# The first batch's attention written out in one fixed order (Nyström attention and a gated MLP on one core)

## The chip, the cores and the metric

The kernel runs on one core of one Trainium2 chip. The metric is the device time of one execution in microseconds; less is better. Three runs of the kernel before gave 793.19, 793.43 and 793.94 us, a median of 793.43 us. In this document PE is the matrix engine (TensorE), PEld its weight loads, DVE is VectorE, ACT is ScalarE, POOL is GpSimd, and SP issues the DMAs.

## The reference

Eight batches of Nyström attention (8 heads, 576 tokens, head size 64, 32 landmarks) feed a gated MLP over all 4608 tokens.

```python
q_lm = q.reshape(B, H, m, S // m, D).mean(axis=3)      # m = 32 landmarks; k_lm likewise
A = sm(q, k_lm); Bm = sm(q_lm, k_lm); C = sm(q_lm, k)  # sm: softmax over the last axis
Z = Bm.T / (norm1(Bm) * norminf(Bm) + 1e-6)
for _ in range(6):
    Z = 2 * Z - Z @ Bm @ Z                             # Newton steps to a pseudo-inverse
x = (A @ Z @ C @ v)                                    # (B*S) x (H*D) = 4608 x 512
xn = x / sqrt(mean(x * x) + 1e-6) * rms_g              # one factor for each token row
out = (silu(xn @ w_gate) * (xn @ w_val)) @ w_out       # 512 -> 1536 -> 512
```

## The kernel before

**Stages.** Each batch's attention is handled in two groups g of four heads. The names to follow are these. `sums` adds up the landmarks (tile lmT, L574). `front` multiplies the scores (sC, sA), takes their maxima (L612 to L615), the exponentials on ACT (E, L618; eb, L622) and, in its inner `tail`, the sums' reciprocals and the transposed scores tA (L634). `soften` subtracts the row maxima of tA (L650 on DVE, L651 on POOL) and takes the exponential (L652). `weigh` normalises tA and transposes it to AT (L658 to L665). `turn` and `values` multiply by v (pCV, PV, L710). `newton_start` prepares the inverse (with a copy that spreads four sums over 128 columns, L849), `newton_first` and `newton_step` are the starting value and the six Newton steps (PV, L868 and L884; the last writes VF, L882). `newton_weights` makes W and the weights' factor WT. `second` multiplies out the attention (pO), squares it (sq, L953), finds each token's RMS factor with a bit trick and polynomial (L969 to L981), scales AT with it (L987, L989), and splits the result into a high and a low part, an (L991 on ACT, L992 on DVE). an is what the MLP multiplies.

**The MLP.** `mix_weights` folds WT into a pair of weight slices (pM, Mhi, Mlo); `mlp` multiplies them with an (psg, psv, 12 products for each of the two token halves), takes SiLU on ACT (L505), multiplies on DVE (L506) and splits the result h (L510, L511); `outs` multiplies h by w_out (pso). The MLP of the first half of the hidden units runs batch by batch, and the attention of the next two batches is laid between its products.

**The weights.** They come as pieces of 0.5 MB (tiles wraw), are decoded by two ACT passes (L185, L186) and finished by one DVE pass (L190) in `load_next`, one after another. A piece of gate or value weights is a quarter of a pair (tile wgv).

**What sets the order.** PE's order is fixed as written (`keep_in_program_order`). On the other engines a scheduler orders the instructions by data and priority, unless one is told to come after another (`issue_after`). A planner, the Mixer, deals out generators (`opening`, `first_inverse`, `first_second`, `decode`, later `steady`) by a running clock of costs; `until(chunk, n)` places a part of the second batch's attention behind the n-th product of the MLP. For the first batch the two urgent generators run at high priority, and `decode` (L1100) sends weight pieces and the second batch's first sums between them. `steady` places `sums(1, 1)`, that is the landmark sums of the second batch's second group, behind product 37 and behind the last weight piece finished until then (`early.last`, L796), and `front(1, 1)` behind product 46.

## Time and profile before

| | us |
|---|---|
| median of three runs | 793.43 |
| the profiled execution, whole | 792.78 |
| its span, first to last instruction | 791.0 |
| PE busy in the span | 767.7 (97%) |
| DVE, ACT, POOL busy | 567.5, 418.6, 182.1 |

The page of the profile gives the chain that ended last as 87% PE, with 4% DVE, 4% ACT and 2% DMA. All timeline times below are microseconds from the start of the span. "Idle before" in square brackets is the time in which the engine stood still before a row's instruction, with what ended it. Instructions in a row overlap a little: the distance from one start to the next is what a queue pays for one.

### The profile page before, as it was taken

The page shows a single profiled execution, that of the slowest core. Times are in us where ns is not written, and L with a number is a line of the kernel's source. Part 1 is how long each engine was busy: PE and PEld are TensorE (multiplying, and loading weights), DVE is VectorE, ACT ScalarE, POOL GpSimd, SP SyncE. Part 2 cuts the span into 40 slices and gives each one's busy share as a digit, 9 for nine tenths or more (in the row PEclk, how much of TensorE's full clock was granted, in tenths as well). Part 3 has the DMA queues.
Part 4 walks back from the last instruction along what each step waited for, and adds up shares of the span by engine and source line. Part 5 has one row for each costly group of instructions (what it writes and reads, how often), then busy time and mean ns, then how long its engine had stood idle before and what let it go on. Part 6 is the DMA issues. An engine that isn't in the chain of part 4 may idle for free.

```text
span 791.0 us, 17865 instructions
## 1 busy us (share of the span) xinstructions
PE 767.7 (97%) x7012; PEld 618.7 (78%) x7012; DVE 567.5 (72%) x1329; ACT 418.6 (53%) x923; POOL 182.1 (23%) x189
## 2 busy tenths in 40 slices
PE   7787999999999999999999999999999999999998
PEld 5465668778778778677778879797979797979796
DVE  7899787947969758688577574767576757766672
ACT  4578465535545455454474785555355444535450
POOL 1005220110210200200200004353334424433430
PEclk9999999999999999999999999999999999999999
DMA  9877461541652532621556541323332424151412
GB/s 320 310 241 221 142 220 61 189 133 33 198 180 93 183 130 70 191 80 53 167 168 211 168 137 41 132 94 145 94 145 68 158 80 159 54 184 56 171 41 80
DMA packets 55204, 110.83 MB, mean 140 GB/s; under 512 B 5456, under 2 KB 29008, under 8 KB 55120
## 3 DMA queue, kind: packets, MB, share of 16 engines
q1 hardware_dynamic: 55120, 109.69, 41.5%
q8 instruction: 55, 0.90, 0.5%
q14 instruction: 29, 0.24, 0.1%
HBM read 73.69 MB, written 35.98 MB: 139 GB/s over the span
## 4 chain that ended last, share of the span: by engine, by line
PE 87%; DVE 4%; ACT 4%; DMA 2%; issue 2%; SPq 0%; ACTq 0%; DVEq 0%
PE pso L115 38%; PE p L115 17%; PE psg L115 8%; PE psv L115 8%; PE pM L115 5%; PE pn L115 2%; PE pCV L115 2%; PE sC L115 2%; PE pO L115 1%; PE pss L115 1%; DMA qk<-in_k_dram 1%; PE sE L121 1%; DMA wrawo<-in_moe_w_out_dram 1%; PE pW L115 1%; DVE lmT L574 1%
## 5 line engine op out<-in xcount | busy, mean ns | idle before, releaser
L115 PE MATMUL pso<-wo,h 128*128 128x512 f32 x648 | 158.4, 396 | 0.0
L115 PEld LDWEIGHTS pso<-wo,h 128*128 128x128 f32 x648 | 118.6, 188 | 31.4 <-ACT E L618 4.2
L115 PE MATMUL pso<-lhio,h 128*128 128x512 f32 x432 | 139.2, 392 | 0.0
L115 PEld LDWEIGHTS pso<-lhio,h 128*128 128x128 f32 x432 | 81.1, 188 | 23.0 <-issue 5.9
L115 PE MATMUL p<-xb,Bwgv 128*128 128x288 f32 x560 | 90.8, 296 | 0.0
L115 PE MATMUL psg<-an,Mhi 128*128 128x288 f32 x384 | 85.3, 306 | 4.6 <-ACT s L505 2.5
L115 PE MATMUL pso<-lloo,h 128*128 128x512 f32 x216 | 84.4, 391 | 0.0
L115 PE MATMUL psv<-an,Mhi 128*128 128x288 f32 x384 | 83.9, 302 | 0.0
L115 PEld LDWEIGHTS p<-xb,Bwgv 128*128 128x128 f32 x560 | 81.3, 188 | 1.2
L413 POOL TENSOR_TENSOR s<-s,vv 128x576 f32<-128x576 f32 x40 | 57.4, 1434 | 98.5 <-DVE vv L455 95.6
L115 PEld LDWEIGHTS psg<-an,Mhi 128*128 128x128 f32 x384 | 61.9, 189 | 16.5 <-DVE WT L898 4.2
L115 PE MATMUL p<-xb,Bwo 128*128 128x288 f32 x392 | 70.1, 295 | 0.0
L115 PEld LDWEIGHTS psv<-an,Mhi 128*128 128x128 f32 x384 | 62.7, 191 | 2.1
L1123 ACT COPY ob<-pso 128x512 f32<-128x512 f32 x36 | 21.0, 589 | 74.5 <-PE pso L115 53.1
L115 PEld LDWEIGHTS p<-xb,Bwo 128*128 128x128 f32 x392 | 58.9, 188 | 1.2
L115 PE MATMUL psv<-an,Mlo 128*128 128x288 f32 x192 | 59.0, 307 | 0.0
L505 ACT ACTIVATE s<-psg 128x288 f32<-128x288 f32 x96 | 39.4, 410 | 36.0 <-PE psg L115 35.8
L115 PE MATMUL psg<-an,Mlo 128*128 128x288 f32 x192 | 58.3, 304 | 0.0
L651 POOL TENSOR_TENSOR tA<-tA,mA 128x576 f32<-128x576 f32 x16 | 18.3, 1164 | 170.3 <-DVE mA L650 170.3
L1185 DVE TENSOR_TENSOR obl<-obl,pso 128x512 f32<-128x512 f32 x36 | 24.7, 686 | 43.3 <-PE pso L115 43.3
L506 DVE TENSOR_TENSOR s<-s,psv 128x288 f32<-128x288 f32 x96 | 42.4, 446 | 11.0 <-PE psv L115 7.5
L510 ACT CAST h<-s 128x576 fp32r<-128x576 f32 x48 | 32.2, 670 | 28.2 <-DVE s L506 28.2
(185 smaller groups left out, 1479.0 us busy)
## 6 DMA issues: line engine op xcount, KB each, us to landing
xb<-ad SPq DMA_DIRECT2D x16, 1008.0 KB, 5.3
qk<-in_q_dram SPq DMA_DIRECT2D x16, 576.0 KB, 4.8
qk<-in_k_dram SPq DMA_DIRECT2D x16, 576.0 KB, 6.0
pd<-ob SPq DMA_DIRECT2D x36, 256.0 KB, 3.6
ad<-t SPq DMA_DIRECT2D x64, 144.0 KB, 1.8
obl<-pd SPq DMA_DIRECT2D x36, 256.0 KB, 2.7
out_dram<-obl SPq DMA_DIRECT2D x36, 256.0 KB, 2.1
vt<-in_v_dram SPq DMA_DIRECT2D x16, 512.0 KB, 5.7
```

What stands on the lines that cost most here:

```text
L115: tc.keep_in_program_order(nc.tensor.matmul(*args, **kw))
L121: tc.keep_in_program_order(nc.tensor.transpose(*args))
L413: kept(eng.tensor_mul(ss[f][:, e], ss[f][:, e], vv[f][:, e]))
L505: silu["last"] = nc.scalar.activation(s[:, cols], banks[0], AF.Silu).ins
L506: nc.vector.tensor_mul(s[:, cols], s[:, cols], banks[1])
L510: nc.scalar.copy(h[:, 0, TAIL:], s)
L574: fixed["sums", b] = nc.vector.tensor_reduce(lmT[:, z], loaded[b, g][z].rearrange("p h (m c) -> p h m c", c=LM), axis=AX.X, op=ALU.add,)
L651: nc.gpsimd.tensor_sub(tA, tA, mA.unsqueeze(2).broadcast_to([P, NB, M]))
L1123: nc.scalar.copy(ob, ps)
L1185: kept(nc.vector.tensor_add(ob, ob, ps))
```

## The change

**An order by hand.** The generators of the first batch are gone. `opening` now writes the first batch's attention, the first half of the second batch's (`Front(1, 0)`) and the first weight pieces as one list, and every instruction made with `own=pin` keeps its place on its engine's queue. `front` is cut into a class with the parts tops (maxima), exps, totals and turned; `soften` into lower and expose; `weigh` into shares and back; `load_next` into `begin` (the two ACT passes) and the `finish` that it returns (the DVE pass).

**What moves between engines (first batch only).** The scalings of pCV into PV and the copy of W go from DVE to ACT. The normalisation of tA (two multiplications) goes from DVE to POOL. The spreading copy in `newton_start` becomes a reduction over an axis of one element, still on DVE. The four banks of the second token half's pO, pss, pms come from the other PSUM pool.

**What moves in time.** Both groups' maxima come before the sums' reciprocals. The second batch's first sums are cut in two: the q half stands between Newton steps 1 and 2, the k half behind WT. AT is scaled and split by token halves (`row`, `high`, `low`). Six weight pieces pass ACT in the opening, ahead of the first products, where before it was nine; DVE finishes four of them ahead of the second batch's maxima (`tops`) and two behind the split of an. Two more pieces can be fetched ahead (spots wo2 and wo1). The first batch's SiLUs are put behind the last high part of an.

```diff
+        def begin(self, own=free):
...
+            def finish():
+                with tc.issue_after(self.then) if self.then else nullcontext():
+                    last = own(
+                        nc.vector.scalar_tensor_tensor(
+                            w.bitcast(U32),
+                            raw[..., 0].bitcast(U32),
+                            5,
+                            w.bitcast(U32),
+                            op0=ALU.logical_shift_right,
+                            op1=ALU.bitwise_or,
+                        )
+                    )
+                self.last = last.ins
...
-                    silu["last"] = nc.scalar.activation(s[:, cols], banks[0], AF.Silu).ins
+                    with behind(fixed["hi", 0].ins if very else None):
+                        silu["last"] = nc.scalar.activation(s[:, cols], banks[0], AF.Silu).ins
...
+            def turned(self, after=None, es=range(2)):
+                b, g, nt = self.b, self.g, state[self.b]
+                if nt["tA"][g] is None:
+                    nt["tA"][g] = ap.tile([P, NB, M], F32, name="tA", tag="tA", bufs=TAB)
+                with tc.issue_after(after) if after else nullcontext():
+                    for e in es:
+                        fixed["tA", b, g] = self.own(
+                            nc.vector.transpose(
+                                nt["tA"][g][:, e * (NB // 2) : (e + 1) * (NB // 2), :].rearrange("p n m -> p (n m)"),
+                                self.sA[e],
+                            )
+                        )
...
+        def shares(b, g, own=free):
+            tA = state[b]["tA"][g]
+            sumA = sm.tile([P, NB], F32, name="sumA", tag="sumA")
+            own(nc.vector.tensor_reduce(sumA, tA, axis=AX.X, op=ALU.add))
+            own(nc.vector.tensor_scalar_add(sumA, sumA, 1e-9))
+            rA = sm.tile([P, NB], F32, name="rA", tag="rA")
+            own(nc.vector.reciprocal(rA, sumA))
+            own(nc.gpsimd.tensor_mul(tA, tA, rA.unsqueeze(2).broadcast_to([P, NB, M])))
+
+        def back(b, g, own=free):
+            nt = state[b]
+            nt["AT"][g] = AT = ap.tile([P, S], F32, name="AT", tag="AT", bufs=ATB)
+            own(nc.vector.transpose(AT, nt["tA"][g].rearrange("p n m -> p (n m)")))
...
-            nc.vector.tensor_scalar_mul(nt["PV"][:, g, M:], pCV, nt["rs"][g][:, 0:1])
+            to, by = nt["PV"][:, g, M:], nt["rs"][g][:, 0:1]
+            if b:
+                nc.vector.tensor_scalar_mul(to, pCV, by)
+            else:
+                pin(nc.scalar.mul(to, pCV, by))
...
+            b, own = 0, pin
             for g in range(2):
-                sums(0, g, None if g else made.ins)
+                sums(b, g, None if g else made.ins, own=own)
+            one, two = fronts = [Front(b, g, own) for g in range(2)]
+            for _ in range(4):
+                early.fetch()
             for g in range(2):
-                tails.append(front(0, g))
+                load_qk(1, g)
+            for _ in range(4, NF1 + RAWS):
+                early.fetch()
+            for part in fronts:
+                part.tops()
+            for part in fronts:
+                part.exps()
+            one.turned()
+            one.totals()
+            two.turned(es=(0,))
+            two.totals()
+            turn(b, 0, 3, own)
+            turn(b, 1, 0, own)
+            start = newton_start(b, own)
+            BT, den = next(start)
+            p0 = bmm(BT, BT, M, "p0")
             for g in range(2):
-                tails[g](fixed["mx", 0, 1].ins)
-            yield 2.6, 0.0
-            for g in range(2):
-                turn(0, g, 4 - 4 * g)
-                soften(0, g)
-                yield 0.65, 0.0
-            for g in range(2):
-                values(0, g, 1 - g)
-                yield 0.85, 0.0
-            stage["front"] = stage["first"] = 0
+                values(b, g, 1 - g)
+                load_v(1, g)
+            for _ in range(2):
+                early.fetch()
+            newton_first(b, p0, den, own)
+            two.turned(es=(1,))
+            lower(b, 0, own=own)
+            newton_step(b, 0, own)
+            spare(2)
+            lower(b, 1, own=own)
+            newton_step(b, 1, own)
+            spare(2)
+            ends = [early.begin(own) for _ in range(2)]
+            expose(b, 0, own)
+            expose(b, 1, own)
+            ends.extend(early.begin(own) for _ in range(2))
+            sums(1, 0, zs=(0,), own=own)
+            newton_step(b, 2, own)
+            spare(2)
+            next(start, None)
+            shares(b, 0, own)
+            newton_step(b, 3, own)
+            spare(2)
+            shares(b, 1, own)
+            newton_step(b, 4, own)
+            spare(2)
+            back(b, 0, own)
+            newton_step(b, 5, own)
+            spare(2)
+            back(b, 1, own)
+            newton_weights(b, own)
+            spare(1)
+            parts = second(b, own)
+            next(parts)
+            sums(1, 0, zs=(1,), own=own)
+            next(parts)
+            ends.extend(early.begin(own) for _ in range(2))
+            for _ in range(4):
+                ends.pop(0)()
+            nxt = Front(1, 0, own)
+            load_qk(2, 0)
+            nxt.tops()
+            nxt.exps()
+            next(parts)
+            nxt.turned(es=(0,))
+            next(parts)
+            low_parts = mix_weights(early, 0, 0, True, own)
+            low_parts()
+            for _ in parts:
+                pass
+            nxt.turned(es=(1,))
+            nxt.totals()
+            for end in ends:
+                end()
+            early.after = fixed["hi", 0].ins
+            for name in ("front", "first", "newton", "wt", "second"):
+                stage[name] = 0
...
+            spread = sums.unsqueeze(2).broadcast_to([P, 4, M])
+            if b:
+                nc.vector.tensor_copy(sb, spread)
+            else:
+                own(nc.vector.tensor_reduce(sb, spread.unsqueeze(3), axis=AX.X, op=ALU.max))
...
+            if b:
+                nc.vector.tensor_copy(W, straight)
+            else:
+                own(nc.scalar.copy(W, straight))
...
-                po = [pa.tile([P, HS], F32, name="pO", tag="pa") for n in range(4)]
+                pool, tag = other if e else (pa, "pa")
+                po = [pool.tile([P, 512], F32, name="pO", tag=tag)[:, :HS] for n in range(4)]
...
+            def row(e, n=1):
+                cols = slice(e * HS, (e + n) * HS)
+                at = slice(e * (NB // 2), (e + n) * (NB // 2))
+                own(nc.vector.transpose(rT[:, cols].rearrange("p (n m) -> p n m", m=M), rb[:, at]))
+                for g in range(2):
+                    own(nc.vector.tensor_mul(ATs[g][:, cols], ATs[g][:, cols], rT[:, cols]))
+
+            def high(g, cols=slice(0, S)):
+                fixed["hi", b] = own(nc.scalar.copy(an[:, 0, g, cols], ATs[g][:, cols]))
+
+            def low(g, cols=slice(0, S)):
+                fixed["an", b] = own(
+                    nc.vector.tensor_sub(an[:, 1, g, cols], ATs[g][:, cols], an[:, 0, g, cols].bitcast(F32))
+                )
+
+            if b:
+                row(0, 2)
+                for g in range(2):
+                    high(g)
+                    low(g)
+            else:
+                for e in range(2):
+                    row(e)
+                    for g in range(2):
+                        high(g, slice(e * HS, (e + 1) * HS))
+                    for g in range(2):
+                        low(g, slice(e * HS, (e + 1) * HS))
+                hold.enter_context(tc.issue_after(fixed["an", 0].ins))
...
-        spots = itertools.chain([(wp, f"h{f}", 1) for f in range(NF1)], ring)
+        spots = itertools.chain(
+            [(wp, f"h{f}", 1) for f in range(NF1)], [(wp, f"wo{n}", 1) for n in (2, 1)], ring
+        )
...
-        def decode():
-            while early.then is None:
-                yield -0.3
-            yield from early.stream(WAIT0, 2)
-            sums(1, 0, early.then)
-            yield -WAIT0
-            early.then = fixed["sums", 1].ins
-            yield from early.stream(WAIT0, 3)
-
-        early.ahead, early.after = 2, fixed["eb", 0, 1].ins
-        mix.add(first_second(), True)
-        mix.add(first_inverse(), True)
-        mix.add(decode())
-        mix.drain(lambda: stage["newton"] >= 0)
-        with tc.issue_after(fixed[0].ins):
-            mix.add(steady())
-            mix.drain(lambda: stage["second"] >= 0)
-            mix.part()
+        opening()
+        early.ahead = 2
+        mix.add(steady())
+        mix.part()
```

**On DVE, in the Newton steps of the first batch.** Before, from the last row ahead of the third Newton step (PV) on:

```order
L190 SCALAR_TENSOR_TENSOR wgv_436<-wrawg_352,wgv_436 128x4x128
L884 SCALAR_TENSOR_TENSOR PV<-PV,pn 128x192
L665 STREAM_TRANSPOSE AT<-tA 128x576
L190 SCALAR_TENSOR_TENSOR wgv_436<-wrawv_354,wgv_436 128x4x128
L884 SCALAR_TENSOR_TENSOR PV<-PV,pn 128x192
L574 TENSOR_REDUCE lmT<-qk_360 128x64
```

Now, from the first step on:

```order
L1031 SCALAR_TENSOR_TENSOR PV<-PV,pn 128x192
L708 TENSOR_REDUCE mA<-tA 128x18
L1031 SCALAR_TENSOR_TENSOR PV<-PV,pn 128x192
L599 TENSOR_REDUCE lmT<-qk_247 128x64
L1031 SCALAR_TENSOR_TENSOR PV<-PV,pn 128x192
L1008 TENSOR_TENSOR Bs<-Bm,nden 128x64
```

The sums lmT of the second batch (L574, now L599) stood behind the fourth step of PV; one of the two now stands ahead of the third.

**On ACT, from the split of an to the first h.** Before:

```order
L991 CAST an<-AT 128x576 x2
L505 ACT_TABLE_LOAD
L505 ACTIVATE s<-psg 128x288
L687 COPY ET<-sE 128x512
L688 COPY EL<-sF 64x128
L505 ACTIVATE s<-psg 128x288 x2
L510 CAST h_740<-s 128x576
L185 ACTIVATE wrawv_751<-wrawv_751 128x512
```

Now:

```order
L1132 CAST an<-AT 128x288 x4
L194 ACTIVATE wrawg_257<-wrawg_257 128x512
L756 COPY ET<-sE 128x512
L196 ACTIVATE wgv_575<-wrawg_257 128x4x128
L757 COPY EL<-sF 64x128
L528 ACT_TABLE_LOAD
L528 ACTIVATE s<-psg 128x288
L194 ACTIVATE wrawv_259<-wrawv_259 128x512
L528 ACTIVATE s<-psg 128x288
L196 ACTIVATE wgv_575<-wrawv_259 128x4x128
L194 ACTIVATE wrawg_261<-wrawg_261 128x512
L533 CAST h_748<-s 128x576
```

Five passes over weight pieces (L194, L196: pieces 257, 259 and 261) now stand among the first SiLUs (L528) and ahead of the first h (L533), where there was none.

**On DVE, from the second pair's last weight pieces to the scores of the second batch's second group.** qk_363 and qk_250 are that group's q and k; its scores are sC in the row `mx<-sC`. Before:

```order
L190 SCALAR_TENSOR_TENSOR wgv_781<-wrawg_374,wgv_781 128x4x128
L506 TENSOR_TENSOR s<-s,psv 128x288
L574 TENSOR_REDUCE lmT<-qk_363 128x64
L506 TENSOR_TENSOR s<-s,psv 128x288
L574 TENSOR_REDUCE lmT<-qk_363 128x64
L511 TENSOR_TENSOR h_740<-s,h_740 128x576
L506 TENSOR_TENSOR s<-s,psv 128x288
L190 SCALAR_TENSOR_TENSOR wgv_781<-wrawv_751,wgv_781 128x4x128
L283 TENSOR_TENSOR Mlo<-pM,Mhi 128x512 x2
L612 TENSOR_REDUCE mx<-sC 128x1
```

Now:

```order
L204 SCALAR_TENSOR_TENSOR wgv_575<-wrawg_257,wgv_575 128x4x128
L529 TENSOR_TENSOR s<-s,psv 128x288 x2
L204 SCALAR_TENSOR_TENSOR wgv_575<-wrawv_259,wgv_575 128x4x128
L534 TENSOR_TENSOR h_748<-s,h_748 128x576
L204 SCALAR_TENSOR_TENSOR wgv_756<-wrawg_261,wgv_756 128x4x128
L529 TENSOR_TENSOR s<-s,psv 128x288
L305 TENSOR_TENSOR Mlo<-pM,Mhi 128x512 x2
L204 SCALAR_TENSOR_TENSOR wgv_756<-wrawv_398,wgv_756 128x4x128
L599 TENSOR_REDUCE lmT<-qk_250 128x64 x2
L204 SCALAR_TENSOR_TENSOR wgv_756<-wrawg_400,wgv_756 128x4x128
```

The two sums lmT stood behind the first and the second product s; now they stand behind three products, three finished pieces and the low parts of the mixed weights, Mlo.

## Rows read from the trace of the kernel before

**Rows 1.** Windows table: us, busy us (x) by engine, granted clock, DMA share, GB/s

```profile
0.00:44.11 44.11, 31.41 (x465) 20.91 (x465) 34.47 (x96) 23.90 (x58) 4.75 (x14) 1.00 0.86 299
44.11:47.65 3.54, 3.35 (x13) 3.03 (x14) 3.54 (x6) 2.21 (x3) 0.00 (x0) 0.52 0.66 234
...
60.95:63.50 2.55, 0.09 (x1) 0.00 (x1) 2.55 (x9) 2.52 (x5) 0.35 (x2) 1.00 0.92 337
63.50:67.90 4.40, 4.40 (x68) 3.56 (x68) 4.38 (x15) 3.90 (x9) 1.55 (x3) 0.63 0.46 137
...
102.50:791.00 688.50, 683.87 (x5948) 558.60 (x5937) 482.43 (x1121) 354.10 (x783) 160.78 (x155) 1.00 0.37 124
```

**Rows 2.** Timeline, DVE: start us, us, engine, line, operation, shape, count [idle before]

```profile
17.82 1.12 DVE L849 COPY nsb<-nsum 128x128 f32<-128x128 f32 x1
...
20.39 0.23 DVE L868 TENSOR_TENSOR PV<-p,nden 128x64 f32<-128x64 f32 x1
...
25.50 0.35 DVE L884 SCALAR_TENSOR_TENSOR PV<-PV,pn 128x192 f32<-128x192 f32 x1
...
30.08 0.47 DVE L882 SCALAR_TENSOR_TENSOR VF<-PV,pn 128x128 f32<-128x128 f32 x2
...
35.84 0.46 DVE L612 TENSOR_REDUCE mx<-sC 128x1 f32<-128x288 f32 x1 [2.96 <-PE sA L115]
...
42.05 1.43 DVE L989 TENSOR_TENSOR AT<-AT,rT 128x576 f32<-128x576 f32 x2
...
64.47 0.87 DVE L857 TENSOR_TENSOR nden<-nnm 128x2 f32<-128x2 f32 x1
```

**Rows 3.** Timeline, DMA queue of SP

```profile
12.42 0.87 SPq L561 DMA_DIRECT2D qk<-in_q_dram  x1
```

**Rows 4.** DMA issues in 12.3 to 13.3 us: count, KB, us to landing

```profile
qk<-in_q_dram SPq DMA_DIRECT2D x1, 576.0 KB, 9.2
```

**Rows 5.** Timeline, ACT

```profile
32.78 1.32 ACT L953 ACTIVATE sq<-pO 128x288 f32<-128x288 f32 x4 [3.93 <-PE pO L115]
...
35.49 0.70 ACT L185 ACTIVATE wrawv<-wrawv 128x512 f32<-128x512 int8 x1
...
40.01 0.50 ACT L618 ACTIVATE E<-sC,mx 128x288 f32<-128x288 f32 x1
...
43.37 1.25 ACT L991 CAST an<-AT 128x576 fp32r<-128x576 f32 x2
...
57.28 1.28 ACT L618 ACT_TABLE_LOAD   x1 [1.42 <-DVE mx L615]
```

**Rows 6.** Timeline, PE

```profile
32.01 2.84 PE L115 MATMUL pO<-AT,W 32*64 32x288 f32 x32 [0.16 <-DVE W L897]
...
44.11 0.61 PE L115 MATMUL psg<-an,Mhi 128*128 128x288 f32 x1 [1.26 <-ACT an L991]
...
54.01 0.43 PE L115 MATMUL sC<-qk,lmT 64*32 64x288 f32 x1
...
63.50 0.53 PE L115 MATMUL psg<-an,Mhi 128*128 128x288 f32 x2 [2.46 <-ACT s L505]
...
68.40 1.09 PE L115 MATMUL pM<-wgv,WT 64*32 64x512 f32 x16
```

**Rows 7.** Groups by line, DVE, 21 to 60 us: xcount | busy us, mean ns

```profile
L574 DVE TENSOR_REDUCE lmT<-qk 128x64 f32<-128x1152 f32 x4 | 5.4, 1344 | 0.0
...
L190 DVE SCALAR_TENSOR_TENSOR wgv<-wrawg,wgv 128x512 uint32<-128x512 uint32 x6 | 4.1, 681 | 0.0
```

**Rows 8.** Groups by line, ACT, 35 to 60 us

```profile
L281 ACT CAST Mhi<-pM 128x512 fp32r<-128x512 f32 x4 | 2.1, 593 | 0.0
...
L505 ACT ACTIVATE s<-psg 128x288 f32<-128x288 f32 x4 | 1.7, 416 | 1.9 <-PE psg L115 1.9
```

**Rows 9.** Timeline, POOL

```profile
16.59 2.28 POOL L651 TENSOR_TENSOR tA<-tA,mA 128x576 f32<-128x576 f32 x2 [3.20 <-DVE mA L650]
...
64.16 1.16 POOL L663 TENSOR_TENSOR tA<-tA,rA 128x576 f32<-128x576 f32 x1 [2.10 <-ACT EL L688]
```

More of the change, by code (lines that the diff above doesn't have):

```diff
@@ L273, in mixed_banks, with mix_weights @@
         return ps
-    def mix_weights(wts, b, pair, late=False):
+    def mix_weights(wts, b, pair, late=False, own=free):
         ps = mixed_banks(wts, b, pair)
@@ L280, in mix_weights @@
         for g in range(G):
-            nc.scalar.copy(hi[:, g], ps[g])
+            own(nc.scalar.copy(hi[:, g], ps[g]))
             if not late:
@@ L288, in low_parts @@
                 mm(ps[g], minus, hi[:, g], start=False, stop=True, skip_group_check=True)
-                nc.scalar.copy(lo[:, g], ps[g])
+                own(nc.scalar.copy(lo[:, g], ps[g]))
         return low_parts
@@ L568, in load_v, with sums @@
             loaded[b, g, "v"] = (vt, vt2)
-        def sums(b, g, after=None):
-            lms[b, g] = lmT = sm.tile([P, 2, 2, M], F32, name="lmT", tag="lmT", bufs=2)
+        def sums(b, g, after=None, zs=range(2), own=free):
+            if (b, g) not in lms:
+                lms[b, g] = sm.tile([P, 2, 2, M], F32, name="lmT", tag="lmT", bufs=2)
             with tc.issue_after(after) if after else nullcontext():
-                for z in range(2):
-                    fixed["sums", b] = nc.vector.tensor_reduce(
-                        lmT[:, z],
-                        loaded[b, g][z].rearrange("p h (m c) -> p h m c", c=LM),
-                        axis=AX.X,
-                        op=ALU.add,
-                    )
@@ new lines, in sums, with __init__, tops @@
+                for z in zs:
+                    fixed["sums", b] = own(
+                        nc.vector.tensor_reduce(
+                            lms[b, g][:, z],
+                            loaded[b, g][z].rearrange("p h (m c) -> p h m c", c=LM),
+                            axis=AX.X,
+                            op=ALU.add,
+                        )
+                    )
+        class Front:
+            def __init__(self, b, g, own=free):
+                self.b, self.g, self.own = b, g, own
+                lmT, qk = lms.pop((b, g)), loaded.pop((b, g))
+                pool, tag = (pa, "pa") if b or not g else (pg, "pg")
+                sC = [pool.tile([P, 512], F32, name="sC", tag=tag) for e in range(2)]
+                sA = [pool.tile([P, 512], F32, name="sA", tag=tag) for e in range(2)]
+                for e in range(2):
+                    for h in range(4):
+                        for z, bank, at in ((1, sC[e], rho(g, h)), (0, sA[e], pos(g, h))):
+                            mm(
+                                bank[rows(at), :HS],
+                                lmT[half(h), 1 - z, h // 2, :],
+                                qk[z][half(h), h // 2, e * HS : (e + 1) * HS],
+                                start=True,
+                                stop=True,
+                            )
+                psB = sC[1][:, HS : HS + M]
+                for h in range(4):
+                    mm(
+                        psB[rows(rho(g, h)), :],
+                        lmT[half(h), 0, h // 2, :],
+                        lmT[half(h), 1, h // 2, :],
+                        start=True,
+                        stop=True,
+                    )
+                self.sC = [s[:, :HS] for s in sC]
+                self.sA = [s[:, :HS] for s in sA]
+                self.psB = psB
+                self.mx = sm.tile([P, 3], F32, name="mx", tag="mx")
+                self.ss = sm.tile([P, 3], F32, name="ss", tag="ss")
+                self.rs = sm.tile([P, 2], F32, name="rs", tag="rs")
+            def tops(self, after=None):
+                mx, own = self.mx, self.own
@@ L648, in soften, with front, lower @@
+        def front(b, g, after=None, late=None):
+            made = Front(b, g)
+            made.tops(after)
+            made.exps()
+            made.totals()
+            made.turned(late or after)
+        def lower(b, g, after=None, own=free):
+            tA = state[b]["tA"][g]
             mA = sm.tile([P, NB], F32, name="mA", tag="mA")
             with tc.issue_after(after) if after else nullcontext():
-                nc.vector.tensor_reduce(mA, tA, axis=AX.X, op=ALU.max)
-            nc.gpsimd.tensor_sub(tA, tA, mA.unsqueeze(2).broadcast_to([P, NB, M]))
@@ L652, in soften @@
[L652 to L666 removed]
+                own(nc.vector.tensor_reduce(mA, tA, axis=AX.X, op=ALU.max))
@@ L674, in spare, with turn @@
             idle(pg.tile([P, 512], F32, name="psw", tag="pg")[:, :P], n)
-        def turn(b, g, more=0):
+        def turn(b, g, more=0, own=free):
             E = state[b]["E"][g]
@@ L686, in turn @@
             EL = ap.tile([2 * M, P], F32, name="EL", tag="EL", bufs=2)
-            nc.scalar.copy(ET, sE)
-            last = nc.scalar.copy(EL, sF)
+            own(nc.scalar.copy(ET, sE))
+            last = own(nc.scalar.copy(EL, sF))
             if (b, g) == (1, 1):
@@ L938, in nystrom_moe_kernel, with second @@
         fixed = {}
-        def second(b):
+        def second(b, own=free):
             nt = state.pop(b)
             W, ATs = nt["W"], nt["AT"]
+            other = (pa, "pa") if b else (pg, "pg")
             sqs = []
```

328 lines of the change are left out of this document (130 added, 198 removed).

## The prediction

> **What bounds the kernel now.** I read the windows table first, since a share of 97% over the span says little about a change that is all in the first tenth of it. From 102.50 us to the end PE is busy 683.87 of 688.50 us at a granted clock of 1.00 [rows 1]. The order of PE's instructions behind that point is the same in both kernels, so what the change is worth is how much earlier or later PE gets there. Up to 44.11 us PE only serves the first batch's attention (31.41 us busy, most of it small products and fillers), and the first product of the MLP, psg, starts at 44.11 [rows 6]. From there PE is dense, with three blemishes that the reader finds in the same table: 44.11 to 47.65 at a clock of 0.52, a standstill of 2.46 us that ends at 63.50, and 63.50 to 67.90 at 0.63 [rows 1, 6]. Granted levels are 1.2 and 2.4 GHz; 0.52 is nearly all at the lower one. The standstill has its cause on ACT: the exponentials of the second batch's second group wait for its maxima, then load their table (1.28 us, from 57.28 on), and the SiLU that frees psg stands behind them [rows 5, 6].
>
> So I ask two questions: when does psg start now, and which wait between 44 and 68 us ends last then. I followed each engine's queue in the new order, with durations and pitches from the trace of before.
>
> **Part 1, up to the first psg.** Before, the six Newton updates pace this part: the start value PV at 20.39, the third update at 25.50, the sixth (VF) at 30.08, so 1.53 us each at the end [rows 2]. Three things ahead of the start value go: two scalings of pCV move to an idle ACT, the reductions of tA move behind it, and the copy nsb, 1.12 us for 128 columns, becomes a reduction that doesn't wait for POOL. The start comes 0 to 2.9 us earlier; from the rows around the copy I take 2.0 or more. Then the q half of the second batch's sums, now pinned ahead of the third update, decides: q is issued at 12.42 and takes 9.2 us to land [rows 3, 4], so 21.6, and the sum takes 1.34 [rows 7]. The third update starts at 22.95 in place of 25.50. If the start value doesn't come earlier, this gain is nil; if the transfer lands sooner, it is 2.9 at most. VF follows at 22.95 + 3 x 1.53 = 27.5 (before 30.08).
>
> From VF to the first square, sq, it was 2.70 us (30.08 to 32.78) [rows 2, 5], with the copy W on DVE; on an idle ACT it costs its own length only, and DVE has two finishes fewer in the way: 2.5, so 30.0. Eight squares take 2.7 (32.78 to 35.49), to 32.7. Before, eight decoding passes stood behind them on ACT, 35.49 to 40.01, so 0.565 a pass; four stand there now, to 35.0. From the first exponential E at 40.01 to the first high part of an at 43.37 it was 3.36 [rows 5]: ACT is ready at 38.3. DVE is the later one. The k half of the sums and four finishes of 0.68 [rows 7] lie ahead of the maxima mx, which start at 33.3 (before 35.84). From mx to an it was 43.37 - 35.84 = 7.53; half of the scaling (1.43 for two [rows 2]), half of the transposition rT, one transposition tA and the second batch's reciprocals now stand behind the first half of an, which I put at 1.8 together: 33.3 + 5.7 = 39.0, and the first psg at 39.5. **That is 4.6 us earlier than 44.11.** The normalisation on POOL has slack here: AT stands behind the fifth update now.
>
> About the POOL work the row shows this: the copy nsb ended at 18.94, when a subtraction pair on POOL (16.59 + 2.28) ended too, and nden, a product of two columns, took 0.87 us from 64.47 on and ended at 65.34, within 0.02 of a POOL multiplication [rows 2, 9]. The Trainium skill, "SBUF — State Buffer", section "Who interferes with whom", says that a DVE copy or scalar operation in a two-port mode, or one with two inputs in SBUF, and GpSimd exclude each other for a whole instruction, and that a tensor_reduce never contends on trn2; the trace agrees. By that rule the reduction nsb is free, but the normalisation of the first group on POOL may hold up the second group's small sumA operation. The sum would be up to 0.4 higher (most of one 1.16 us multiplication is covered by the sums ahead). I leave it out of the sum and keep 0 to 1.16 in the range.
>
> **Part 2, from psg to the scores of the second group.** Before, this stretch had 44.11 to 54.01 with no wait on PE. The scores sC and sA of the second batch's second group need two landmark sums, and these now stand on DVE behind finishes whose passes have yet to run on ACT. From the first 12 products (39.5 to 42.6, at half clock as before) and the turn of E, ET can be copied at 43.4. From there ACT's queue to the last pass that the sums wait for is: ET and EL 0.65, a table load 1.28, eight passes at 0.565, 4.52, three SiLUs with some 0.95 between starts in all (0.42 each alone), one h 0.57, two Mhi 1.06 (0.59 each alone) [rows 5, 8]. That is 9.0, so 52.5. One finish of 0.68 and two sums of 1.34 on DVE [rows 7] give 55.8, and the scores end at 56.9. Before they started at 54.01 and were done at 55.1. **So here 6.4 us go back: 1.8 later than before.** PE, whose order is fixed, stands still for some 3.4 us ahead of the first scores and 1.3 between those of the q half and the k half. Passes left out of the opening's queue were only postponed into this one. With pitches as long as single durations it would be 0.6 later; if DVE slips the sums in a row or two earlier, up to 1.2 earlier.
>
> **Part 3, from the scores to the next pair's mixing, pM.** Before, this was 55.1 to 68.40, 13.3 us, of which 2.46 were the standstill and 4.40 x 0.37 = 1.6 the lower clock; 9.2 were work. Now five SiLUs stand ahead of the exponentials' table load, four before. The fifth frees a bank for six products, about 1.0 us at full clock; 1.4 of the standstill stays. Behind the standstill of part 2 I expect the lower clock once, as after 44.11, where 3.54 at 0.52 lost 1.7. That is 9.2 + 1.4 + 1.7 = 12.3, and pM at 69.2 in place of 68.40: +0.8. Until 102.5 DVE has one finish (0.68) fewer in the queue; half of it I take as reaching PE, -0.3.
>
> **The sum.** -4.6 + 6.4 - 1.0 - 0.3 = +0.5 against the profiled execution's 792.78 us (its span is 791.0, and 1.8 lie around it). The median of the runs is 793.43, 0.65 more. So 792.78 + 0.5 + 0.65 = 793.9. If the first twelve products run at full clock, psg being nearer to the fillers, 1.0 goes; the bounds on POOL add up to 1.16.
>
> **The rivals.** First, *the standstill moves and the old ones vanish* (faster). The wait of 2.46 at the table load exists because DVE's maxima came late; with the scores already delayed PE may have enough SiLU results, and the stretch at 0.63 need not follow. Then part 3 is 9.2 + 1.7 - 0.6 in place of 12.3, about 2.0 less, and with a start value at its better bound (0.3 to 0.5) and a pass or two passed over (up to 0.6) it is 3.0 less: 790.9. For it: the four engines are all dense there and ACT's rows leave no gap. Against it: the exponentials still stand between two SiLUs.
>
> Second, *the second group's sums on DVE become the bound* (slower). Place: the two sums behind the last needed pass. Price: the standstill of 4.7 on PE, the lower clock behind it (1.7), and the table load's wait as before, 2.46, since the maxima come late by the same amount: 1.0 more than in my sum, and 0.4 to 0.7 from POOL and the finishes: 795.5. It decides from the point where the last pass ends later than about 52.9. For it: the chain of 9.0 has no gap in it. Against it: one more SiLU stands ahead.
>
> Third, *the change gains little in its own part*: the pinned sum holds DVE until q has landed, and with two more pieces fetched ahead q lands later than 21.6. Each us of it moves all behind, as no cover is left; 3 us would give 797. Windows before 44.11 have DMA at 0.86 [rows 1], so it can be; q's place in SP's queue is the same, which speaks against it.
>
> **How the numbers follow.** I give the forecast 0.42, the first rival 0.29, the second 0.22, the third 0.07. What can be told from no change is 0.2%, 1.6 us, so 791.8 to 795.0. Faster: 0.27 of the first rival and 0.03 of the forecast's spread, 0.30. Slower: 0.19 of the second, 0.07 of the third and 0.03 of the forecast, 0.29. Same: 0.41. The forecast's own range is 792.3 to 795.0; the range that holds 8 in 10 reaches to the first rival's better half and over the second: 789.8 to 796.4.
>
> **What would show it.** Right: in the changed profile the third update starts near 23 and VF near 27.5; psg starts near 39.5; ACT runs without a gap from there to about 52; PE has a wait of 3 us or more that the lmT sums end, ahead of sC at 54 to 56, and a granted clock near 0.5 behind it; pM within 1 us of 69.2; and behind 102.5 both traces run in step. Wrong: psg later than 41 (part 1), no such wait ahead of sC (part 2), or no wait for a SiLU behind the table load (part 3).

## The result, and the profile after

The changed kernel takes 800.83 us (median of 4 runs, 799.21 to 801.51) against 793.31 us for the kernel before (4 runs in all, 792.36 to 793.94). The ratio is 1.0093, 95% interval 1.0074 to 1.0111: slower by some 7.4 us, where 793.9 was forecast and 796.4 was the upper end of the range. The profiled execution took 800.62 us, its span is 798.8.

The windows table of the profile after (start:end, then us, busy us (x instructions) of PE, PEld, DVE, ACT, POOL, the granted clock, DMA share, GB/s), cut at its own events:

```profile
18.41:22.16 3.75, 0.00 (x0) 0.00 (x0) 0.30 (x1) 3.08 (x6) 1.16 (x1) 1.00 1.02 405
22.16:25.80 3.64, 3.64 (x38) 2.81 (x38) 1.85 (x4) 0.45 (x1) 1.16 (x1) 0.53 1.04 380
39.40:49.70 10.30, 8.61 (x44) 6.67 (x29) 8.24 (x25) 6.54 (x17) 0.00 (x0) 0.51 0.58 215
55.90:60.28 4.38, 0.67 (x2) 0.13 (x2) 4.38 (x6) 3.12 (x6) 0.00 (x0) 0.95 0.67 211
73.50:83.80 10.30, 9.42 (x72) 6.25 (x69) 8.61 (x15) 8.58 (x16) 6.73 (x9) 0.50 0.54 157
112.00:798.80 686.80, 682.09 (x5929) 556.91 (x5927) 481.10 (x1114) 353.86 (x783) 160.79 (x155) 1.00 0.37 123
```

The last row is the same dense stretch as in [rows 1]: nothing was lost there (PE stands idle for 4.71 us of it, for 4.63 in the window before). Ahead of it stand two windows in which PE does next to nothing (18.41 and 55.90) and three at the lower clock level of 1.2 GHz, 24 us together, where [rows 1] has 3.54 and 4.40 us. One caution on that comparison: the profiled execution of the kernel before has a mean granted clock of 0.996 over its span, the one of the changed kernel 0.982; 93 other executions of the kernel before have 0.984 to 0.995.

PE's timeline after (start us, us, engine, line, operation, shape, count, [idle before <- what ended it]); the psg and pM of [rows 6] are among its rows:

```profile
18.06 0.35 PE L115 MATMUL pn<-PV 32*32 32x96 f32 x2
22.16 0.79 PE L115 MATMUL pn<-PV 32*32 32x96 f32 x14 [3.75 <-issue]
...
43.34 1.10 PE L115 MATMUL psg<-an,Mhi 128*128 128x288 f32 x2 [1.01 <-ACT an L1132]
...
59.03 0.67 PE L115 MATMUL sC<-qk,lmT 64*32 64x288 f32 x2 [3.14 <-DVE lmT L599]
60.28 0.68 PE L115 MATMUL sA<-qk,lmT 64*32 64x288 f32 x1 [0.59 <-DVE lmT L599]
...
62.21 0.34 PE L115 MATMUL sC<-lmT 64*32 64x32 f32 x6
...
73.50 1.96 PE L115 MATMUL pM<-wgv,WT 64*32 64x512 f32 x16
...
99.08 0.29 PE L115 MATMUL pms<-sqT,sel 128*128 128x18 f32 x2
```

And DVE's, to be held against [rows 2]:

```profile
17.46 0.22 DVE L1014 TENSOR_TENSOR PV<-p,nden 128x64 f32<-128x64 f32 x1
...
23.06 0.35 DVE L1031 SCALAR_TENSOR_TENSOR PV<-PV,pn 128x192 f32<-128x192 f32 x1 [4.35 <-issue]
...
26.50 0.34 DVE L1031 SCALAR_TENSOR_TENSOR PV<-PV,pn 128x192 f32<-128x192 f32 x1
...
29.14 0.46 DVE L723 TENSOR_SCALAR sumA<-sumA 128x18 f32<-128x18 f32 x1
...
30.71 0.45 DVE L1029 SCALAR_TENSOR_TENSOR VF<-PV,pn 128x128 f32<-128x128 f32 x2
...
57.63 2.60 DVE L599 TENSOR_REDUCE lmT<-qk 128x64 f32<-128x1152 f32 x2
```

The start value PV came 2.93 us earlier (17.46), and then PE stood, and DVE behind it. The first Newton product pn is 16 instructions in the trace; PE ran two and stopped at 18.41 for 3.75 us with no semaphore in sight ("issue"), in the middle of a group whose data were there: the last of them, the second scaling of pCV on ACT, ended at 18.51. ACT's timeline:

```profile
18.20 0.31 ACT L783 ACTIVATE PV<-pCV,rs 128x64 f32<-128x64 f32 x1 [0.55 <-PE pCV L115]
```

Both traces have one packet of 16 KB on queue q8 ("instruction") close to that: between 16.5 and 17.0 us before, between 19.5 and 20.0 after. In the DMA view of these half microseconds (queue: packets, MB, share of 16 engines) it reads, before and after:

```profile
q8 instruction: 1, 0.02, 14.1%
```

```profile
q8 instruction: 1, 0.02, 13.6%
```

In both PE goes on some 2.5 us behind the start of the packet, at 22.16 after. The kernel before stood too, but 1.28 us and ahead of filler products, while DVE still worked on PV (20.39); PE's timeline before:

```profile
17.61 0.33 PE L115 MATMUL p<-BT 32*32 32x32 f32 x16
19.21 1.16 PE L115 MATMUL psw<-ident 128*128 128x128 f32 x8 [1.28 <-issue]
20.67 0.53 PE L115 MATMUL pn<-PV 32*32 32x96 f32 x16 [0.30 <-DVE PV L868]
```

Both kernels stop at the same place of PE's stream. Windows that begin at 0 and end within the standstill count the same 218 products (the x behind PE's busy time), before and after:

```profile
0.00:18.60 18.60, 14.07 (x218) 10.31 (x218) 13.38 (x36) 8.07 (x22) 3.18 (x10) 1.00 0.93 314
```

```profile
0.00:20.00 20.00, 13.21 (x218) 9.72 (x218) 13.67 (x40) 7.51 (x23) 2.32 (x9) 1.00 0.91 318
```

In the old order the 218th is the last product of p; in the new order it is the second of pn.

### The profile page after: what moved, and what is told of

Read it like the earlier page. It is cut to its first block, busy times and chain, and to the rows that moved or that the text cites. A ratio compares the mean times of both kernels' runs of the same rounds, so it can differ in the third digit from the quotient of the medians.

```text
span 798.8 us, 17861 instructions
## 1 busy us (share of the span) xinstructions
PE 772.2 (97%) x7002; PEld 621.4 (78%) x7002; DVE 568.1 (71%) x1329; ACT 420.0 (53%) x928; POOL 184.1 (23%) x191
## 4 chain that ended last, share of the span: by engine, by line
PE 90%; DVE 4%; ACT 3%; issue 1%; DMA 1%; SPq 0%; ACTq 0%
PE pso L115 38%; PE p L115 17%; PE psg L115 9%; PE psv L115 9%; PE pM L115 5%; PE pn L115 3%; PE sC L115 2%; PE pCV L115 2%; PE pO L115 1%; PE pW L115 1%; DMA qk<-in_k_dram 1%; DVE lmT L599 1%; PE pss L115 1%; PE sE L128 1%; PE sA L115 1%
## 5 line engine op out<-in xcount | busy, mean ns | idle before, releaser
L115 PEld LDWEIGHTS psg<-an,Mhi 128*128 128x128 f32 x384 | 63.5, 194 | 15.9 <-DVE WT L1049 5.0
L528 ACT ACTIVATE s<-psg 128x288 f32<-128x288 f32 x96 | 39.4, 410 | 40.5 <-PE psg L115 40.2
L533 ACT CAST h<-s 128x576 fp32r<-128x576 f32 x48 | 32.2, 670 | 28.3 <-DVE s L529 28.3
```

What stands on the lines that cost most here:

```text
L115: tc.keep_in_program_order(nc.tensor.matmul(*args, **kw))
L528: silu["last"] = nc.scalar.activation(s[:, cols], banks[0], AF.Silu).ins
L533: nc.scalar.copy(h[:, 0, TAIL:], s)
```

## The experiments

Three theories, to be told apart: **A**, PE's standstill ahead of the second group's scores is DVE's late sums, and costs by itself; **B**, PE stood inside pn for its own instructions, which arrive behind the weights; **C**, the stretches at half clock behind the standstills cost time of their own. "Ratio" is always to the kernel before on the same chip; the changed kernel has 1.0093.

**A alone.** In `opening`, and out of `steady`:

```diff
             for end in ends:
                 end()
+            sums(1, 1, own=own)
...
-            sums(1, 1, early.last)
```

> The changed kernel with one edit: the two landmark sums of the second batch's second group stand on DVE right behind the finishes at the end of the opening, no longer behind the last weight piece (early.last). Theory A (PE's standstill ahead of the second group's scores is DVE's late sums): the wait of some 4.5 us ahead of sC goes, sC starts within 1 us of the product ahead of it (near 56.5 in place of 60.3), and the time falls by 4 to 6 us, to 795 to 797. Rival (ACT's eight passes are the bound and the sums only ended last): PE stands still at another place by about as much, at pM or psg, and the time falls by less than 1.5 us.

796.05 us, ratio 1.0028 (1.0015 to 1.0040), some 5 us less. The sums run at 49.14 and the scores end at 57.26 in place of 62.55. DVE's and PE's rows:

```profile
49.14 2.61 DVE L599 TENSOR_REDUCE lmT<-qk 128x64 f32<-128x1152 f32 x2
```

```profile
57.00 0.26 PE L115 MATMUL sC<-lmT 64*32 64x32 f32 x8
```

A holds as to the cause of the wait. "By itself" is not shown: with the wait some of the low clock behind it went, too (the span's mean clock rises from 0.982 to 0.987).

**B, the traffic.** The third and later weight pieces, the second group's q and k and the next v wait for the start value (a small memset of one raw tile behind PV holds the queue):

```diff
+            newton_first(b, p0, den, own)
+            for n in range(2, NF1 + RAWS):
+                early.fetch(n == 2)
+            load_qk(1, 1)
...
-            newton_first(b, p0, den, own)
```

> The changed kernel with fewer transfers under way at 15 to 20 us: the weight pieces from the third on, the second group's q and k and the v of the second batch are issued only behind the Newton starting value (17.5 us). Theory B (PE stood still 3.75 us inside the first Newton product because its own instructions, 16 KB on queue q8, arrived behind the weights): the wait shrinks below 1.5 us, the second PV update starts near 21 in place of 23.06, psg by 41.5 in place of 43.34, and the time falls by 2 to 4 us, to 797 to 799. Rival (the wait has to do with the semaphores of PV or the new engine of the scaling): it stays at 3.5 us or more and the time is within 1 us of 800.8.

798.94 us, ratio 1.0064 (1.0046 to 1.0082): 2.3 us less. Same place, half the wait, the packet at 17.5 to 18.0 us; the second update comes at 21.11, as expected, psg at 42.44, 0.9 later than expected. PE's timeline:

```profile
17.94 0.35 PE L115 MATMUL pn<-PV 32*32 32x96 f32 x2
20.13 0.86 PE L115 MATMUL pn<-PV 32*32 32x96 f32 x14 [1.84 <-issue]
```

The wait was expected under 1.5 us, so the traffic has a part in it, and B was too hopeful about the cure.

**B, the place.**

```diff
-            turn(b, 1, 0, own)
+            turn(b, 1, 6, own)
```

> The changed kernel with six filler products more (12 instructions of the trace) in a gap of PE ahead of the Newton start. Theory B (a boundary in PE's instruction stream): the standstill begins at the same instruction number, so 12 instructions further ahead in the program, inside the second pCV and not inside pn; its end, near 22, hardly moves, and the time is within 1 us of 800.8. Rival (something pn waits for): the standstill stays inside pn, behind its first product.

798.70 us, ratio 1.0065 (1.0053 to 1.0077). The standstill moved into the second pCV; PE's timeline:

```profile
17.16 0.65 PE L115 MATMUL pCV<-vt,ET 128*32 128x64 f32 x31
19.63 0.24 PE L115 MATMUL pCV<-vt,ET 128*32 128x64 f32 x1 [1.83 <-issue]
19.81 0.32 PE L115 MATMUL pCV<-vl,EL 64*32 64x64 f32 x8
```

From two of pn's back to 31 of 32 of the vt products is 2 + 8 + 1 = 11 instructions, for twelve put in ahead: PE stops behind 219 products in place of 218. The place is a number in PE's instruction stream, not a wait of pn. Not expected were that it ended 2.5 us earlier, with the packet at 17.0 to 17.5, and that the time fell by 2.2 us: how far PE has come seems to count for the packet, too.

**A and B together** (first and second edit):

> The edits of the first two together. If A and B are both right they add up: psg by 41.5, sC without a wait, 6 to 9 us less than the changed kernel, so 792 to 795, about the kernel before. By the rivals of both: 799 or more. In between (796 to 798) one of the two waits covers the other.

793.52 us, ratio 0.9997 (0.9987 to 1.0007). The parts add up: some 5.2 and 2.3 alone, 7.6 together. psg starts at 41.27, 2.8 us ahead of [rows 6], and the time is that of the kernel before. PE's timeline:

```profile
41.27 1.10 PE L115 MATMUL psg<-an,Mhi 128*128 128x288 f32 x2 [1.01 <-ACT an L1137]
```

**C, in the changed kernel as it is.** Filler products in PE's waits, no wait removed:

```diff
+            if not b:
+                idle(room[:, 2 * P : 3 * P], 5)
...
+                idle(fixed["room"][:, 2 * P : 3 * P], 2 if g == 0 else 0)
...
+            idle(fixed["room"][:, 2 * P : 3 * P], 3)
...
+            spare(14)
             front(1, 1)
```

> The changed kernel as it is, with filler products in PE's waits alone: ten at 36 to 43 us and fourteen (some 3.8 us) ahead of the second group's scores, where PE stands still for the sums. Theory C: the stretches at half clock, 27 us in all in the changed kernel against 7 before, get shorter by 10 us or more and the time falls by 2 to 4 us, to 797 to 799, though no wait is taken away. Rival (the low clock lies where others set the pace): within 1 us of 800.8, or slower by the fillers' own length.

796.55 us, ratio 1.0039 (1.0026 to 1.0052), 4.3 us less for work that nobody needs. Its windows (columns as above):

```profile
36.50:46.00 9.50, 8.51 (x72) 6.01 (x62) 8.43 (x29) 7.63 (x20) 0.00 (x0) 1.00 0.64 229
46.00:56.00 10.00, 7.23 (x59) 5.61 (x58) 8.05 (x18) 9.89 (x20) 0.68 (x1) 1.00 0.45 155
56.00:60.00 4.00, 4.00 (x62) 3.32 (x61) 4.00 (x6) 1.37 (x2) 0.00 (x0) 1.00 0.44 131
```

The clock stays at 1.00 from 36.5 to 60, the scores end at 59.75 in place of 62.55, though psg starts only 0.36 earlier. The mean granted clock of the span goes from 0.982 to 0.991.

**C, in the kernel before** (nineteen fillers: `idle` 7 and 4 ahead of the low parts and of psg, and `turn(b, 1, 8)`):

> The kernel before with filler products alone, nineteen of them: in PE's waits for Mhi and an (40 to 44 us) and behind the turn of E ahead of the wait of 2.46 us at 63.5. Theory C: the two stretches at half clock (3.4 us each) go and the time falls by 1 to 2.5 us, to 791 to 792.5. Rival (the clock hits there what others pace): within 0.6 us of the kernel before, or slower by up to 1 us where a filler stands in the way.

793.30 us, ratio 0.9998 (0.9990 to 1.0007). Here the rival is right. The window of the first products, from their first to the turn sE:

```profile
43.79:47.29 3.50, 2.50 (x15) 1.84 (x14) 2.87 (x6) 3.18 (x5) 0.00 (x0) 1.00 0.70 253
```

Full clock where [rows 1] had 0.52, and the stretch takes 3.50 us against 3.54: PE now waits between the products, for an from DVE and ACT, 1.0 us in three waits (0.40, 0.22 and 0.39). In these two kernels a low clock cost time where PE was the late engine, and none where others were.

The executions on record point the same way, since the mean granted clock of one and the same kernel differs from one to the next. The four of the changed kernel had 0.980, 0.981, 0.982 and 0.989 and took 801.51, 801.04, 800.62 and 799.21 us. Of the twelve with A's edit alone, eleven had 0.982 to 0.989 and took 795.46 to 797.17; one had 0.996 and took 790.77. In the kernel before the effect is small: 27 executions at 0.988 or less have a median of 793.87, 13 at 0.993 or more one of 793.01. That is no experiment, since a longer wait may lower the clock as well as the other way round.

**Two more pieces decoded in the opening**, with the first and third edit:

```diff
+            ends.extend(early.begin(own) for _ in range(2))
             newton_step(b, 4, own)
```

> The changed kernel with the early sums, the six filler products more ahead of the Newton start, and two more weight pieces passed on ACT in the gap it has from the fifth Newton update on (eight pieces in the opening in place of six). If ACT's passes between the first SiLUs are a bound of their own beside the late sums (the step of the prediction that counts eight passes there), psg stays near 41.3, the SiLUs come 2 us earlier behind it, PE's waits for ACT s up to the second pM shrink from some 1.9 to under 1 us, and the time is 789.5 to 792. Rival: with the sums out of the way ACT has slack, and the time is that of the two edits alone, 793 to 795.

797.01 us, ratio 1.0045 (1.0033 to 1.0058), 3 to 4 us worse than the two edits would add up to. PE's waits for s up to the second pM didn't shrink (1.64 and 0.35 us), so the theory that ACT's passes bound them found no support. ACT's queue, free sooner, took the next pieces (w_out) ahead of the table load that the exponentials wait for. ACT's timeline:

```profile
58.31 0.68 ACT L194 ACTIVATE wrawo<-wrawo 128x512 f32<-128x512 int8 x1 [1.66 <-DMA wrawo<-in_moe_w_out_dram]
59.02 0.67 ACT L196 ACTIVATE w<-wrawo 128x512 int32<-128x512 f32 x1
59.65 0.68 ACT L194 ACTIVATE wrawo<-wrawo 128x512 f32<-128x512 int8 x1
60.35 1.28 ACT L659 ACT_TABLE_LOAD   x1
61.64 0.50 ACT L659 ACTIVATE E<-sC,mx 128x288 f32<-128x288 f32 x1
```

Its first pass waits 1.66 us for a transfer with the table load behind it in line. PE waits 2.58 us for E. Two kernels built on it told little. With the ten fillers:

> As the one before, with ten filler products on PE in its three waits from 36 to 41 us (for sqT, Mhi and an). Theory C (the stretches at half clock behind PE's standstills cost by themselves): the granted clock from psg on is 1.0, the first twelve products take 2 us in place of 3.5, and the time is 1 to 2 us less than without them. Rival (ACT and DVE set the pace there and a slower PE costs nothing): within 0.6 us of the one before.

797.99 us, ratio 1.0059 (1.0045 to 1.0072): inconclusive, since this base had lost no clock at 36 to 43 us. With six fillers more at the very start:

> As the one before, with six filler products more at the very start. Theory B has the boundary in PE's instructions another 12 instructions earlier in the program, inside the first pCV; the standstill, 1.83 us with the shift of 12, gets shorter or falls where PE waits anyway, and psg starts 0.5 to 1.8 us earlier; time 788 to 791. Rival (the instructions' landing is a matter of the transfers ahead of them alone): the standstill ends at the same time, near 19.7, and psg stays within 0.4 us.

797.57 us, ratio 1.0047 (1.0033 to 1.0061). The boundary moved on by twelve products, still inside the second pCV, and the standstill stayed (1.87 us, its end at 19.59): moving it further gained nothing.

**The normalisation back on DVE** (`nc.vector` for b = 0 in `shares`):

> The changed kernel with the first batch's normalisation back on DVE, the rest as it is. If the move to POOL was worth what DVE is spared (two of 0.75 us in the Newton updates, which DVE paces): VF 0.5 to 1.5 us later, time 0 to 1.5 us more than 800.8. Rival of the prediction (POOL and DVE hold each other up, 0.4 us or more): the second group's sumA operation, 0.46 us with POOL at work, takes 0.17 to 0.26, VF is not later, time the same or up to 0.5 less.

801.75 us, ratio 1.0104 (1.0089 to 1.0118), against 1.0093 (1.0074 to 1.0111) unclear as a whole. In its trace VF starts at 31.92 (30.71 with POOL), and the sumA operation takes 0.17 us in place of 0.46. So POOL did hold it up by 0.3 us, and the move was still worth 1.2 us at VF.

**All three cures** (first, second and the ten fillers):

> The changed kernel with the early sums, the later issue of the weight pieces and the filler products in PE's three waits from 36 to 43 us. If A, B and C are right and each takes its own part, the first twelve products run at full clock, the stretches at half clock fall to 10 us or less, and the time is 790 to 792, below the kernel before. Rival (as in the kernel with two more pieces, a faster start only collides on ACT and DVE ahead of the second Newton start): 793 to 795, with a longer wait for PV near 68.

792.83 us, ratio 0.9997 (0.9989 to 1.0006), the ratio of A and B together. The rival came nearer: the longer wait for PV is there, 3.17 us ahead of 67.62. So the 4.3 us that fillers brought in the changed kernel are no part beside A's and B's: the three gains overlap. With the third edit too:

> As the one before, with the six filler products more ahead of the Newton start. Theory B in full (both the place of the boundary and the traffic count): the standstill for instructions gets shorter than the 1.8 us that either edit alone leaves, by 1 us or more, and the time is up to 1.5 us less than without. Rival (1.8 us is the least that a landing costs here): the standstill stays near 1.8 us and the time within 0.6 us.

793.50 us, ratio 1.0002 (0.9991 to 1.0012), the standstill 2.02 us. The least that any version of the changed kernel paid is 1.75 us. One regularity stands in all sixteen traces: PE goes on 2.4 to 2.6 us after the packet starts. The packet starts 1.3 us before PE stops in the kernel before, 0.6 to 0.8 before in every version with the later transfers or with the six fillers ahead, and 0.9 to 1.3 after it in the four that have neither; the standstill is the difference.

Where did the rest of the time go? DVE's timeline in the kernel with the three cures:

```profile
65.16 0.69 DVE L1015 TENSOR_TENSOR Bs<-Bm,nden 128x64 f32<-128x64 f32 x1
65.77 1.66 DVE L208 SCALAR_TENSOR_TENSOR w<-wrawo,w 128x512 uint32<-128x512 uint32 x1
67.35 0.21 DVE L1021 TENSOR_TENSOR PV<-p,nden 128x64 f32<-128x64 f32 x1
```

beside POOL's:

```profile
64.61 2.27 POOL L731 TENSOR_TENSOR tA<-tA,rA 128x576 f32<-128x576 f32 x2 [2.48 <-DVE sumA L728]
66.82 1.51 POOL L1017 COPY blocks<-Bs 32x64 f32<-32x64 f32 x4
```

PE waits 3.17 us for this PV. **PV put first** (Bs and the finish of the first w_out piece behind it):

```diff
+                if kind == "o" and "waits" in stage:
+                    stage["waits"].append(finish)
...
+            if b == 1:
+                next(stage["start"], None)
+                for finish in stage.pop("waits"):
+                    finish()
```

> The changed kernel with the three cures (early sums, later pieces, fillers) and, on DVE, the second Newton start's PV put ahead of two instructions that stood before it and met POOL's multiplications there: Bs (0.69 us in place of 0.22) and the finish of the first piece of w_out (1.66 us in place of 0.68). If these two hold the 3.2 us that PE waits for PV at 67.6, that wait falls to 1.5 us or less, PE gets to the second batch's weights pW 1 to 2 us earlier than 80.3, and the time is 790.5 to 792, below the kernel before. Rival (the next thing on DVE or ACT, the finish or the low parts, then ends as late for the pM behind it): pW at 80 or later and the time within 0.6 us of 792.8.

793.95 us, ratio 1.0002 (0.9993 to 1.0011). The wait fell to 0.97 us, and the second pM started at 65.20, 3.2 us ahead of [rows 6]; then PE waited 2.01 us for a SiLU and ran at a clock of 0.53 from 69.0 to 76.0, and pW came at 81.31. PE's timeline and the window:

```profile
64.74 0.53 PE L115 MATMUL pn<-PV 32*32 32x96 f32 x16 [0.97 <-DVE PV L1031]
65.20 1.09 PE L115 MATMUL pM<-wgv,WT 64*32 64x512 f32 x16
```

```profile
69.00:76.00 7.00, 5.94 (x49) 4.63 (x48) 4.93 (x10) 4.09 (x9) 3.70 (x4) 0.53 0.62 176
```

**Five fillers in that wait:**

```diff
                         mix_weights(wts, b, pairs[n + 1])
+                        if n:
+                            idle(fixed["bank"][:, 3 * P :], 5)
```

> As the one before (three cures, PV first), with five filler products behind the second group's mixing pM, in PE's wait of 2.0 us for a SiLU at 68.3. If the 3.2 us that PV first gained at pM (65.2 against 68.4) are lost to the 6.8 us at half clock that follow the waits at 66 to 70, the clock stays at 1.0 there, pW comes at 78 to 79.5 in place of 81.3, and the time is 790.5 to 792. Rival (the Newton updates are paced by DVE whatever PE's clock): pW within 0.7 us of 81.3 and the time within 0.6 us of 793.5.

792.48 us, ratio 0.9986 (0.9977 to 0.9994): the one version that beats both kernels, the kernel before by some 1 us. Its clock there is 1.00, and pW comes at 80.08, 1.2 us earlier where 1.8 to 3.3 were expected. PE's waits on the way are now for DVE (0.77 us for PV, 1.03 for s, 0.46 for VF).

## Why the prediction was wrong

- **Part 1, the step that failed:** "the q half of the second batch's sums, now pinned ahead of the third update, decides". The start value came as early as its better bound had it, and q was not waited for. PE's own instructions decided, a wait that the sum put at nothing: 3.75 us inside pn, ahead of the first update. The third update stood at 26.50 in place of 22.95, psg at 43.34 in place of 39.5. The rest of the part was right in sum to 0.3 us (psg is 3.84 late, of which 3.55 stand at the update already). The trace before had the row, 1.28 us of "issue" at 19.21, in a wait that the change took away; I didn't ask what that wait covered. The third rival had the place and nearly the price (3 us, 797), and the wrong cause.
- **Part 2:** right in kind. PE stood for the two sums, 3.14 and 0.59 us (3.4 and 1.3 forecast); A took it away. The stretch was 1.8 us longer (19.2 us from psg to the end of the scores, 17.4 forecast). Of these, some 1.2 lie in the scores themselves: behind the second sum they ran at half clock from 60.28 to 62.55, 2.3 us where 1.1 had been counted. ACT's chain was 0.5 us too short, and not without a gap: it waited 1.44 us for AT and 1.28 for sE.
- **Part 3:** 11.0 us in place of 12.3 up to pM, 1.3 less, for two reasons. Most of the low clock that it counts (1.7) fell on the scores, a part earlier. And the 1.4 us for a SiLU behind the exponentials' table load didn't come, which was one of the signs of being wrong: PE waited for no SiLU between the scores and pM, but 1.41 us for DVE's PV at 73.04. So a wait of the same size stood there for another reason, and that the term fits is luck.
- **Behind pM** I let the loss end, with -0.3. From pM to pms it took 25.6 us, before 23.3 (pM in [rows 6], pms below), with 10.3 us at 0.50, a stretch for which the sum had no term. PE is busy for 24.70 us of it, before for 21.34, so it was late there by its clock. That the clock alone costs the 2.3 us is not shown: the version with five fillers has 1.00 all along and takes 24.5 us. PE's timeline before:

```profile
91.66 0.29 PE L115 MATMUL pms<-sqT,sel 128*128 128x18 f32 x2
```

- The sum: 3.8 + 1.8 - 1.3 + 2.6 = 6.9 us more than forecast at pms; the execution is 7.3 over its own forecast of 793.3.
- The POOL term kept in the range was measured at 0.3 us, well inside it. The first rival was right about its place: the wait of 2.46 and the low clock behind it are gone, and 11.0 us is nearer to its 10.3 than to 12.3; part 1 buried it. The second rival's condition held (the last pass ended at 56.84, not by 52.9), mostly through part 1, but the wait of 2.46 in its price didn't come.
- One reading was short: the first twelve products "as before" got 3.1 us, where [rows 1] has 3.54.

**What is not settled:** what makes the packet of instructions start, and so why no version of the changed kernel got the standstill under 1.75 us. The runs show that the traffic and the instructions ahead of it both move its start. That the packet holds PE's code is argued from the place and the times; the profile names only its queue.

## What to carry to other kernels

A short wait marked "issue" on an engine may be code in flight. Here it stood behind the same number of products in the old order and the new, so count them. Before taking away the wait that covers it, see what would then stand in its place, and keep the transfers of the first stretch no earlier than they are needed. Follow the clock behind every standstill that a change makes, but price it only where that engine is the late one; a few idle products in the wait were worth 4.3 us in one kernel here, nothing in another, and nothing more once the waits were gone. Work pulled out of a queue's path makes room for the next work of a planner, which may be worse.

## What the runs showed of the hardware

- Behind its 218th or 219th product, whatever the order, PE stood and went on 2.4 to 2.6 us after a 16 KB packet on q8 had started: 1.28 us in the kernel before, 3.75 in the changed one, 1.84 and 1.83 with one cure each, at DMA shares of 1.09, 1.02, 0.85 and 1.06. Over the span of the changed kernel q8 has 55 packets and 0.90 MB; no other wait of PE marked "issue" is over 0.62 us. The Trainium skill, "Runtime: NRT & Kernel Launch", section "Instruction fetch mechanics", has the blocks of 16 KB and calls the cost of crossing one mostly hidden. The traces agree for the other packets and disagree for this one.
- Beside POOL's multiplication a DVE operation with two inputs in SBUF took 1.66 us where its mean is 0.68 [rows 7], and a small one 0.69 (0.22 in the changed kernel). That is the exclusion that the Trainium skill, "SBUF — State Buffer", section "Who interferes with whom", states; here it is a whole-instruction price on a path that PE waits for.
